# Attention with a threshold, then a squared-ReLU MLP: GpSimd issues the writes of turned blocks, and one piece of MLP work changes sides of the values

## The chip, the cores and the metric

The kernel runs on one core of a Trainium2 chip. The metric is the device time of one execution in microseconds (us). A core has these engines, each with an instruction stream of its own: TensorE (PE in the profile, its weight loads PEld) multiplies matrices, VectorE (DVE) and ScalarE (ACT) do elementwise work and read PSUM, GpSimd (POOL) does elementwise work in SBUF, and SyncE (SP) here only issues DMAs. ACT and POOL can issue DMAs too. Every engine works through its instructions in order, and an instruction that waits holds up everything behind it on its engine.

## The reference

There are 8 batches with 8 heads, 576 tokens and 64 values per head. Each row of scores keeps only the entries within tau of its maximum. The result goes through a two-layer MLP, 512 to 2048 to 512, over all 4608 tokens.

```python
scores = scale * np.matmul(q, k.transpose(0, 1, 3, 2))
thresh = np.max(scores, axis=-1, keepdims=True) - tau
scores = np.where(scores >= thresh, scores, -1000000000.0)
scores = scores - np.max(scores, axis=-1, keepdims=True)
attn = np.exp(scores)
attn = attn / (np.sum(attn, axis=-1, keepdims=True) + 1e-09)
attn_out = np.matmul(attn, v)
x = attn_out.transpose(0, 2, 1, 3).reshape(B * S, H * D)
r = np.maximum(x @ w_in, 0.0)
out = (r * r) @ w_out
```

Everything is float32.

## The kernel before

**Visits and steps.** Two heads of a batch are worked on together; this is a *visit*. There are 36 visits, numbered from 0: the four head pairs of the first batch come twice (a part of the queries each time), the other 28 once. A visit goes through blocks of 128 queries; one block is one *step*. From visit 12 on, visits come in pairs (an even and an odd one) that share nine steps: first a block made of the 64 left-over queries of both, then blocks 0 to 3 of the even visit, then blocks 0 to 3 of the odd one. The odd visit is the "second visit" of the change's description.

**One step.** TensorE computes the scores into PSUM (L289). VectorE takes the row maxima (L310), ScalarE the exponents (L322 to L325), VectorE applies the threshold and sums (L337 to L340), GpSimd divides (L345 and L347) in SBUF.

**Values.** The product with v (`mix`, L502) needs the weights with keys on the partitions. From visit 11 on this is done in three moves. `turn_blocks` transposes 32x32 blocks on VectorE into the tile `turned` (L431 to L441), one step after the weights were divided. For two blocks of queries together `set_aside` (L408) writes 1152 KB of `turned` to `aside`, a buffer in HBM. `place_blocks` reads it back with four DMAs of SP (L449) so that each 32x32 block lies at its place in the tile `wT`. The blocks of left-over queries go from `turned` to `wT` directly (L458, L466). So each full visit has two writes and eight placements; there are 50 writes and 200 placements in all. Only then can the values of the visit be computed: for an even visit four steps after its last step, for an odd one three steps after. The values go to PSUM bank 0 (first group) and bank 4 (second group); the second group needs the blocks that were placed last. ACT copies both banks to `xT` (the puts, L485 to L496).

**MLP.** Work on chunks of 256 tokens is cut into *pieces*, which wait in a queue and fill TensorE between attention steps: `piece()` takes the next one. In chunks from the third on both layers use seven products of half-size blocks instead of eight; L659 is the first layer (`unit`), L765 the second (`product`). Sums and differences of weight blocks for these are made by GpSimd and VectorE (L590), others of tokens by GpSimd (L636), the evictions by ACT and VectorE (among them L671, L691, L803). GpSimd issues the stores of the output (L743).

**Order.** The order on every engine is the program's order, written out by hand. `late_step` is one step of the stretch with pairs. It emits the scores, maxima and exponents; then, if the block turned in this step is the second of two, its transposes and, through `turn_last`, the write. Then come some pieces (`fill` takes them by an estimated share of time), threshold and division, loads, and in a step that has values (`valued`) the three things at issue: `at_least(1, made)` makes sure that a piece lies between what went before and the values, `values()` emits them, and after the placements and further fills `at_least(2, made)` makes sure that two pieces lie between the values and the next scores.

The DMAs that SP issues stand in one order too: loads of q, k and v for later visits (L201), placements (L449, L458, L466).

Of the kernel before, what the change touches and what calls it, by code (L numbers as in the profile page):

```python
# [19 lines left out]
def kernel(  # L20
# [10 lines left out]
    nc = tc.nc  # L31
# [62 lines left out]
    NB = 2 * KB * 2 * 32  # L94
    turned = const.tile([P, 2 * NB], FP32, name="turned")
# [102 lines left out]
    def some_loads():  # L198
        for _ in range(min(1 + (len(loads) > 8), len(loads))):
            to, src = loads.popleft()  # L200
            nc.sync.dma_start(out=to, in_=src)  # L201
# [75 lines left out]
    def area(u, odd):  # L277
        at = AT[u, odd][0]
        return big[:, at:at + S].rearrange("p (h k) -> p h k", h=2)

    def scores_of_two(s):


        vis, i = steps[s]

        def term(u, odd, second_part, lhsT, keys, to=slice(0, P)):
            at, cut = AT[u, odd]
            x0, x1 = (cut, S) if second_part else (0, cut)
            nc.tensor.matmul(big[to, at + x0:at + x1], lhsT, keys[u * D:(u + 1) * D, x0:x1], start=True, stop=True)  # L289

        if i == NBLK:
            for x in range(2):
                for v_ in range(2):
                    for u in range(2):
                        cols = slice(v_ * D, (v_ + 1) * D)
                        term(u, 0, x != u, qmid[u * D:(u + 1) * D, cols], kT[v_], cols)
            return
        for at_, (u, odd, x) in enumerate(((1, 1, 0), (0, 0, 0), (1, 0, 1), (0, 0, 1), (1, 0, 0), (0, 1, 0), (1, 1, 1), (0, 1, 1))):
            at = (i + odd) * P
            term(u, odd, x, qT[u * D:(u + 1) * D, at:at + P], kT[vis % 2])  # L300
            if at_ == 0:
                nc.scalar.copy(seen, big[:, AT[1, 1][0]:AT[1, 1][0] + 1])

    def maxima(s, sc):
        vis, i = steps[s]
        n = len(sc)
        st = stats[s % len(stats)]
        mx = st[:, 0, 0:n]
        for u in range(n):
            nc.vector.tensor_reduce(out=mx[:, u:u + 1], in_=sc[u], axis=AX.XY, op=ALU.max)  # L310
        w = w_slots[(s - first_dma) % (2 if by_dma(vis) else 3)][:, 0:n, :]
        weights[vis, i] = w, sc, st
# [6 lines left out]
    def exponents(vis, i):  # L319
        w, sc, st = weights[vis, i]  # L320
        mx, thr, bias = (st[:, j, 0:len(sc)] for j in range(3))
        nc.scalar.activation(out=bias, in_=mx, func=AF.Copy, scale=-SCALE)  # L322
        nc.scalar.activation(out=thr, in_=mx, func=AF.Identity, bias=ntau8)  # L323
        for u in range(len(sc)):
            nc.scalar.activation(out=w[:, u, :].rearrange("p (h k) -> p h k", h=2), in_=sc[u],  # L325
                                 func=AF.Exp, bias=bias[:, u:u + 1], scale=SCALE)
# [78 lines left out]
    def set_aside(vis, pair):  # L405

        t = aside[len(outside) % 4]
        nc.scalar.dma_start(out=t, in_=turned[:, 0:NB])  # L408
        outside[vis, pair] = t.rearrange("(b r) (j x) -> r j b x", r=32, j=4)

    def turn_blocks(vis, i):
# [31 lines left out]
    def place_blocks(vis, pair, which=range(4)):  # L443

        wb = blocks[vis, pair]
        if pair < NBLK // 2:
            for j in range(4):
                g0 = (ONE, TWO)[pair] // REST
                nc.sync.dma_start(out=wT[j * 32:j * 32 + 32, g0:g0 + 4, :, :].rearrange("r b c q -> r b (c q)"),  # L449
                                  in_=outside[vis, pair][:, j, :, :])  # L450
            return
        for qb in which:
            rows = slice(qb * 32, qb * 32 + 32)
            for j in range(4):
                to = wT[j * 32:j * 32 + 32, :, :, :]
                at = slice(qb % 2 * 32, qb % 2 * 32 + 32)
                if paired(vis):
                    nc.sync.dma_start(out=to[:, (LEFT if qb < 2 else ODD) // REST, :, at], in_=wb[rows, j:2 * KB:4, :])  # L458
                else:


                    first = j if qb < 2 else KB + (j - KB) % 4
                    n = len(range(first, KB if qb < 2 else 2 * KB, 4))
                    c = first // 4
                    first += 2 if qb < 2 else -KB
                    nc.sync.dma_start(out=to[:, LEFT // REST, c:c + n, at], in_=wb[rows, first:first + 4 * n - 3:4, :])  # L466
# [152 lines left out]
    def some_later(engine):  # L619
        if later[engine]:  # L620
            make(*later[engine].popleft())
# [212 lines left out]
    mixes = {}  # L834
# [46 lines left out]
    def add_chunk(j):  # L881
        waiting.extend(pieces_of(j))
        whole.add(j)
# [23 lines left out]
    def after():  # L907
        now = state["last"]
        state["last"] = []
        for fn in state["then"]:  # L910
            state["last"] += fn() or []
        state["then"] = []
        for fn in now:
            fn()

    def piece():
        _, fn, *what = waiting.popleft()
        state["left"] -= PIECE_US
        state["made"] += 1
        if fn is mlp_out or what[0] <= PLAIN and what[1] == 0:  # L920
            after()
        then = fn(*what)
        after()
        state["then"] = then
        if state["step"] >= NST:
            some_later("vector")
            some_later("gpsimd")

    def fill(us):
        state["left"] += us  # L930
        while waiting and state["left"] >= PIECE_US / 2 and waiting[0][0] <= state["usable"]:
            piece()
        state["left"] = min(state["left"], PIECE_US)
# [75 lines left out]
    def turn_last(s):  # L1009
        if s <= NST:  # L1010
            turn_blocks(*steps[s - 1])
            n, i = steps[s - 1]
            if i % 2 and by_dma(n) and goes_out(n, i // 2):
                set_aside(n, i // 2)

    def goes_out(n, pair):

        return pair < NBLK // 2

    def at_least(count, made):  # L1020
        while waiting and state["made"] < made + count:
            piece()

    def late_step(s):

        on = s < NST
        odd = on and steps[s][1] % 2 == 1
        if on:
            n, i = steps[s]
            if not odd:  # L1030
                scores_of_two(s)
            after()
            maxima(s, [area(u, odd) for u in range(2)])
            some_later("gpsimd")
            exponents(n, i)
        first = s > NST or steps[s - 1][1] % 2 == 1 or steps[s - 1][1] == NBLK
        if first:
            turn_last(s)
        valued = s in mixes and s < END

        todo = list(place_at[s])

        def place(all_):
            for what in list(todo):
                if all_ or not goes_out(*what[:2]):
                    place_blocks(*what)
                    todo.remove(what)

        if not valued:
            place(False)  # L1050

        def values():
            if s in mixes:
                while (visits[mixes[s][0]][0] // HP + 1) * S - RING > read_to["x"]:
                    piece()
                mix(*mixes[s])
                for j in chunk_at.get(s, ()):
                    add_chunk(j)

        if s == END:  # L1060
            values()
        quarter = rate(s) / 4 if s < END else 1e9
        made = state["made"]
        fill(quarter)
        some_later("gpsimd")
        after()
        if on:
            threshold(n, i)
            divide(n, i)
        if first:  # L1070
            some_later("vector")
        fill(quarter)
        after()
        if not first:
            some_later("vector")
            turn_last(s)
        for fn in prep_at[s] + load_at[s]:
            fn()
        some_later("gpsimd")
        if valued:  # L1080
            at_least(1, made)
            made = state["made"]
            values()
        some_loads()
        place(True)
        some_later("vector")
        some_loads()
        fill(quarter)
        some_loads()
        fill(quarter)  # L1090
        some_loads()
        if valued:
            at_least(2, made)
            state["left"] = max(state["left"], -PIECE_US / 2)

    for s in range(END + 1):
        state["step"] = s
        if s >= first_late:
            assert 4 not in kept.values()
            late_step(s)  # L1100
            continue
# [137 lines left out]
```

## Time and profile before

| what | value |
|---|---|
| median of 3 runs | 1334.41 us (1334.23 to 1335.61) |
| the profiled execution | 1334.19 us, of which the span of its instructions is 1332.4 us |
| mean granted clock of TensorE | 0.995 |
| writes of turned blocks (L408, ACT queue) | 50 of 1152.0 KB, median 5.2 us from issue to landing |
| placements (L449, SP queue) | 200 of 288.0 KB, median 5.5 us to landing |
| stores of the output (L743, POOL queue) | 32 of 256.0 KB, median 3.3 us to landing |
| HBM read and written | 133 GB/s over the span |

How to read what follows. A row of the timeline has the start, the length, the engine, the line, what is written and read, and how many instructions were merged; a bracket at its end tells how long the engine was idle before it and what ended the wait. A row of waits reads: engine and line, what it waited for, the total in us, how often, the longest. A row of the windows has, for each stretch, the busy time and the number of instructions of each engine, the clock, the DMA engines' share and GB/s. Names with a q (SPq, ACTq) are an engine's sequencer, which issues DMAs. The page's own warning stands: a busy TensorE is not TensorE at its peak, since ends of matmuls are modelled.

### The profile page before, as it was taken

To read this page: it belongs to the slowest core of one execution; us is meant where nothing else is said; L and a number is where in the kernel's file an instruction comes from. 1 tells how busy PE (TensorE), PEld (TensorE's weight loads), DVE (VectorE), ACT (ScalarE), POOL (GpSimd) and SP (SyncE) were. 2 spreads that over 40 slices of the span, in tenths; PEclk is the share of its full clock that TensorE was granted. 3 is DMA by queue.
4 is the path that set the end of the run, shared out by engine and by line. 5 is a ranking of instruction groups with operands and counts; after the bars stand their busy time and mean duration, and the time that the engine had idled before them with its cause. 6 is when DMAs were issued, how large, how long until landed. Compare 5 with 4: busy or idle time off the path is not lost.

```text
span 1332.4 us, 25133 instructions
## 1 busy us (share of the span) xinstructions
PE 1297.2 (97%) x9112; PEld 1078.2 (81%) x9112; DVE 928.2 (70%) x2026; ACT 585.2 (44%) x1357; POOL 758.3 (57%) x865
## 2 busy tenths in 40 slices
PE   7898999999999999999999999999999999999998
PEld 5676556878796979787888888888887888889997
DVE  6877776777787878777786777868687877732131
ACT  4776674235262535343434443444434343422321
POOL 4689875765655555364655554737274737354451
PEclk7999999999999999999999999999999999999999
DMA  8764531647767686867586685758677577430000
GB/s 159 160 152 117 144 91 36 160 93 183 167 177 170 169 195 165 200 141 200 123 186 147 172 192 138 189 108 205 138 181 169 150 180 164 141 91 1 17 17 16
DMA packets 330124, 186.68 MB, mean 140 GB/s; under 512 B 291440, under 2 KB 291472, under 8 KB 323600
## 3 DMA queue, kind: packets, MB, share of 16 engines
q1 hardware_dynamic: 317696, 116.87, 45.0%
q10 hardware_dynamic: 9504, 59.27, 11.2%
q0 software_dynamic: 2800, 8.93, 1.8%
q8 instruction: 72, 1.18, 0.4%
q14 instruction: 52, 0.43, 0.1%
HBM read 109.22 MB, written 68.42 MB: 133 GB/s over the span
## 4 chain that ended last, share of the span: by engine, by line
PE 85%; DVE 5%; ACT 4%; DMA 3%; POOL 2%; issue 1%; SPq 1%; ACTq 0%; DVEq 0%; POOLq 0%
PE big L659 28%; PE big L765 27%; PE big L502 10%; PE big L289 8%; PE big L548 3%; PE big L273 3%; PE big L730 2%; PE big L386 2%; DMA wT<-aside 2%; DVE st L310 1%; DVE w L337 1%; ACT w L325 1%; ACT wT L387 1%; DMA aside<-turned 1%; PE big L266 0%
## 5 line engine op out<-in xcount | busy, mean ns | idle before, releaser
L337 DVE SCALAR_TENSOR_TENSOR w<-big,st,w 128x576 f32<-128x576 f32 x269 | 207.2, 807 | 97.8 <-ACT w L325 97.5
L310 DVE TENSOR_REDUCE st<-big 128x1 f32<-128x576 f32 x288 | 204.3, 748 | 86.2 <-PE big L289 53.5
L347 POOL TENSOR_SCALAR w<-w,st 128x576 f32<-128x576 f32 x269 | 247.4, 929 | 28.0 <-DVE st L340 24.0
L765 PE MATMUL big<-wo,gsum 128*128 128x256 f32 x1088 | 243.8, 382 | 0.0
L345 POOL TENSOR_SCALAR st<-st 128x2 f32<-128x2 f32 (+1 forms) x148 | 36.6, 247 | 358.6 <-DVE w L337 354.2
L765 PEld LDWEIGHTS big<-wo,gsum 128*128 128x128 f32 x1088 | 204.4, 190 | 37.1 <-issue 8.6
L659 PE MATMUL big<-xT,w_in_sb 128*128 128x128 f32 x1536 | 187.3, 277 | 0.8 <-DVE g L671 0.7
L659 PEld LDWEIGHTS big<-xT,w_in_sb 128*128 128x128 f32 x1536 | 178.5, 192 | 9.8 <-issue 7.6
L765 PE MATMUL big<-wo,g 128*128 128x256 f32 x816 | 185.3, 382 | 0.1
L325 ACT ACTIVATE w<-big,st 128x576 f32<-128x576 f32 x269 | 183.8, 734 | 0.2 <-ACT st L323 0.2
L502 PE MATMUL big<-wT,vs 128*64 128x128 f32 (+5 forms) x1700 | 164.8, 355 | 9.7 <-ACT wT L387 4.2
L765 PEld LDWEIGHTS big<-wo,g 128*128 128x128 f32 x816 | 151.6, 190 | 26.1 <-issue 6.5
L502 PEld LDWEIGHTS big<-wT,vs 128*64 128x64 f32 (+1 forms) x1700 | 97.3, 137 | 73.9 <-issue 21.5
L322 ACT ACTIVATE st<-st 128x2 f32<-128x2 f32 (+1 forms) x148 | 30.3, 205 | 263.4 <-DVE st L310 262.2
L671 DVE TENSOR_TENSOR g<-big,g 128x512 f32<-128x512 f32 x96 | 64.8, 677 | 82.3 <-PE big L659 76.4
L289 PE MATMUL big<-kT,qT 64*128 64x320 f32 (+3 forms) x768 | 108.0, 416 | 0.2 <-DVE w L337 0.2
L289 PEld LDWEIGHTS big<-kT,qT 64*128 64x128 f32 x768 | 84.5, 186 | 15.7 <-issue 4.3
L538 POOL TENSOR_TENSOR gsum<-g 128x512 f32<-128x512 f32 x34 | 46.1, 1356 | 81.6 <-ACT g L668 72.1
L667 ACT ACTIVATE g<-g 128x512 f32<-128x512 f32 x96 | 60.3, 628 | 61.0 <-DVE g L671 59.4
L668 ACT ACTIVATE g<-g 128x512 f32<-128x512 f32 x128 | 80.7, 630 | 4.1
L431 DVE STREAM_TRANSPOSE turned<-w 128x512 f32<-128x512 f32 x100 | 70.3, 703 | 3.7 <-DMA aside<-turned 2.6
L437 DVE STREAM_TRANSPOSE turned<-w 128x512 f32<-128x512 f32 x100 | 66.9, 669 | 0.0
(113 smaller groups left out, 1973.2 us busy)
## 6 DMA issues: line engine op xcount, KB each, us to landing
aside<-turned ACTq DMA_DIRECT2D x50, 1152.0 KB, 5.2
wT<-aside SPq DMA_DIRECT2D x200, 288.0 KB, 5.5
vs<-in_v_dram SPq DMA_DIRECT2D x72, 128.0 KB, 4.4
ql<-in_q_dram SPq DMA_DIRECT2D x126, 72.0 KB, 2.9
wo<-in_moe_w_in_dram SPq DMA_DIRECT2D x16, 512.0 KB, 4.8
wo<-in_moe_w_out_dram SPq DMA_DIRECT2D x16, 512.0 KB, 3.7
out_dram<-osb POOLq DMA_DIRECT2D x32, 256.0 KB, 3.3
kl<-in_k_dram SPq DMA_DIRECT2D x113, 72.0 KB, 3.0
```

The lines of the kernel that those rows point to most:

```text
L289: nc.tensor.matmul(big[to, at + x0:at + x1], lhsT, keys[u * D:(u + 1) * D, x0:x1], start=True, stop=True)
L310: nc.vector.tensor_reduce(out=mx[:, u:u + 1], in_=sc[u], axis=AX.XY, op=ALU.max)
L325: nc.scalar.activation(out=w[:, u, :].rearrange("p (h k) -> p h k", h=2), in_=sc[u], func=AF.Exp, bias=bias[:, u:u + 1], scale=SCALE)
L337: nc.vector.scalar_tensor_tensor(out=wu, in0=sc[u], scalar=thr[:, u:u + 1], in1=wu, op0=ALU.is_ge, op1=ALU.mult, accum_out=sm[:, u:u + 1])
L347: nc.gpsimd.tensor_scalar(out=w[:, u, :], in0=w[:, u, :], scalar1=z[:, u:u + 1], scalar2=rcp[:, u:u + 1], op0=ALU.add, op1=ALU.mult)
L431: move(wb[:, 0:h, :, :], whole_[:, 0, :, :, :])
L437: move(wb[:, h + 1:, :, :], whole_[:, 1, :, :, :])
L502: nc.tensor.matmul(ps[u * D:(u + 1) * D, :], vs[n % 2][rows, u * (NBLK + 1) + c, :], wT[rows, at // REST:(at + ps.shape[1]) // REST, NBLK ...
L659: nc.tensor.matmul(to[:, f, :], factor(j, p, q, c)[:, f * P:(f + 1) * P], part[:, c, :], start=(p in "125" and f == 0 and c == 0), stop=(p ...
L668: nc.scalar.activation(out=to, in_=to, func=AF.Square)
L671: nc.vector.tensor_tensor(out=x, in0=to, in1=x, op=ALU.add)
L765: nc.tensor.matmul(to, left[:, f, :], wo[:, slot, f, :], start=(f == 0), stop=(f == HF - 1))
```

## The change

The write of turned blocks is issued by GpSimd instead of ScalarE, at the same place of the program. And in `late_step`, where a step has values, the counts of pieces ahead of and behind them depend on whether the visit is odd: for even visits one piece ahead and two behind, as before; for odd visits (`mixes[s][0] % 2` is 1) two ahead and one behind. `mixes[s]` holds the visit and the query columns whose values step `s` computes.

```diff
     def set_aside(vis, pair):

         t = aside[len(outside) % 4]
-        nc.scalar.dma_start(out=t, in_=turned[:, 0:NB])
+        nc.gpsimd.dma_start(out=t, in_=turned[:, 0:NB])
         outside[vis, pair] = t.rearrange("(b r) (j x) -> r j b x", r=32, j=4)
...
         some_later("gpsimd")
         if valued:
-            at_least(1, made)
+            at_least(1 + mixes[s][0] % 2, made)
             made = state["made"]
             values()
         some_loads()
...
         fill(quarter)
         some_loads()
         if valued:
-            at_least(2, made)
+            at_least(2 - mixes[s][0] % 2, made)
             state["left"] = max(state["left"], -PIECE_US / 2)
```

## The prediction

> **What bounds the kernel now.** I read the page's busy table first, then the table of windows, the timeline around TensorE's waits, and last SP's waits and timeline.
>
> ```profile
> PE 1297.2 (97%) x9112; PEld 1078.2 (81%) x9112; DVE 928.2 (70%) x2026; ACT 585.2 (44%) x1357; POOL 758.3 (57%) x865
> ```
>
> ```profile
> core 0: us, PE busy (x) PEld busy (x) DVE busy (x) ACT busy (x) POOL busy (x), PEclk, DMA share, GB/s
> 243.00:400.00 157.00, 155.50 (x1044) 130.97 (x1044) 122.79 (x271) 65.41 (x153) 98.11 (x110) 1.00 0.67 159
> 400.00:600.00 200.00, 197.21 (x1403) 164.28 (x1400) 157.37 (x354) 83.00 (x196) 112.27 (x132) 1.00 0.73 174
> 600.00:800.00 200.00, 200.00 (x1412) 168.57 (x1413) 151.04 (x336) 84.23 (x194) 112.17 (x130) 1.00 0.71 169
> 800.00:1000.00 200.00, 198.60 (x1395) 170.29 (x1391) 152.00 (x336) 84.05 (x195) 111.99 (x129) 1.00 0.68 160
> 1000.00:1180.00 180.00, 179.84 (x1240) 149.69 (x1239) 131.05 (x288) 70.38 (x164) 98.26 (x113) 1.00 0.66 162
> ```
>
> TensorE is the bound. The change touches only the stretch from 243 us (the first write of turned blocks is issued at 238.8) to 1180 (the last values). There TensorE is idle for 1.50 + 2.79 + 0.00 + 1.40 + 0.16 = 5.85 us of 937. This caps the gain: 5.85 us is 0.44%. POOL is busy for 57% and has room on average. Four of the idle pieces stand before values (L502):
>
> ```profile
> 278.13 4.75 PE L502 MATMUL big<-wT,vs 128*64 128x320 f32 x38 [1.14 <-DMA wT<-turned]
> ...
> 401.56 2.63 PE L502 MATMUL big<-wT,vs 128*64 128x256 f32 x24 [0.26 <-DMA wT<-aside]
> ...
> 425.32 2.63 PE L502 MATMUL big<-wT,vs 128*64 128x256 f32 x24 [1.14 <-DMA wT<-aside]
> 427.88 3.72 PE L765 MATMUL big<-wo,gsum 128*128 128x256 f32 x16
> 431.53 0.92 PE L289 MATMUL big<-kT,qT 64*128 64x256 f32 x4
> ...
> 567.57 2.63 PE L502 MATMUL big<-wT,vs 128*64 128x256 f32 x24 [1.36 <-DMA wT<-aside]
> ```
>
> The brackets are what the change can win: 1.14 + 0.26 + 1.14 + 1.36 = 3.90 us. By the order of the visits these are visits 11, 14, 15 and 19; three are odd. After visit 15's values two pieces of MLP (3.65 us up to the scores at 431.53) stand behind them. Now SP, which places the blocks:
>
> ```profile
> SPq L201 <- DMA aside<-turned: 165.4, 24, 9.7
> SPq L449 <- DMA aside<-turned: 160.4, 15, 31.8
> ...
> SPq L458 <- DMA aside<-turned: 91.1, 11, 9.8
> ```
>
> ```profile
> 449.02 13.36 SPq L201 DMA_DIRECT2D vs<-in_v_dram  x8
> 462.48 0.54 SPq L201 DMA_DIRECT2D kl<-in_k_dram  x1
> 463.06 1.92 SPq L449 DMA_DIRECT2D wT<-aside  x4
> ```
>
> L449 needs the write's data. L201 loads v, k and q and has nothing to do with it; still it waits for it, 165.4 us in 24 waits. In the built program every DMA of SP and ACT takes the next of eight completion semaphores in turn and waits until its last holder has landed; a write sits on one for its whole flight. So the eight v loads take 13.36 us to issue. The write in question was issued at 451.31 and landed 8.78 later, at 460.09, yet its placement starts only at 463.06, behind loads that had been held up.
>
> **What the Trainium skill says.** "DMA: Bandwidth & Descriptors", section "SWDGE vs HWDGE vs iDMA": a DMA from ACT or SP gets its descriptors from hardware, one from GpSimd from software on GpSimd's cores. Section "The descriptor swizzle": a 1 MiB transfer over 128 partitions needs nine read and nine write descriptors per DMA engine. So rows count, not bytes. The trace agrees as far as it goes: output stores from POOL (L743, 128 rows of 2 KB) occupy POOL for 0.56 to 0.60 us. "SBUF — State Buffer", section "SBUF: two separate sides": descriptor writing stalls while VectorE holds the port it shares with GpSimd; in the section "A bandwidth-pool intuition that's wrong" a DMA of some 620 ns alone takes 3100 beside such an operation. No L743 shows that: all 33 lie between 0.56 and 0.80.
>
> **Part 1: the write moves from ACT to GpSimd.**
>
> *Removed from ACT*: 50 issues of 0.33 us, 16 us, on an engine 44% busy: nothing on the path. The write cannot start earlier, since ACT already issues each 0.03 us after the last transpose ends (for instance 411.98 and 412.01).
>
> *Added to POOL*: 50 x 0.6 = 30 us. I compared POOL's state with the end of the transposes for all 50. In 36 POOL is idle then, 34 times with L345 next, which waits for VectorE's threshold still to come; in the other 14 it is in an L590, L539, L559 or L743 that ends within 1.25 us. The tightest POOL work before TensorE is L590 at 910.7 (TensorE waits 0.73 for it at 912.0). The new issue ahead of it falls between POOL's end at 905.53 and the L345 at 906.12, a hole of 0.59. Cost taken: nothing; if that cover fails, up to 0.6 there.
>
> *Later landing*, call it D. Nothing in the trace shows this write from POOL. Nearest rows, output stores of 256 KB near the end of the run, with no other transfers about (first from POOL, then from SP):
>
> ```profile
> L743 POOL DMA_DIRECT2D out_dram<-osb x4: 560/560/560, 1233.3 to 1285.0; - x4
> DMA to landing us min/median/max: 2.3/2.3/2.3
> ...
> L743 SPq DMA_DIRECT2D out_dram<-osb x2: 362/362/362, 1326.9 to 1329.1; - x2
> DMA to landing us min/median/max: 2.0/2.0/2.0
> ```
>
> By the records 2.30 and 2.04 us: D = 0.26. The skill's fit for GpSimd's path (section "Anatomy of one DMA") gives 2.0 + 1.18 MB / 436e3 = 4.7 us for the write's size, an estimate; the quietest writes from ACT take 4.14, so D = 0.56. Upper end: the 2.5 us of the port stall above, with some loss of share beside SP's loads, 3. Lower end 0, as the issue cannot come earlier. I take 0.5.
>
> *Where D lands.* Even visits: SP's loads no longer wait for the write, so the placement starts when the write lands. In all eleven even visits from 12 to 32 the placement started 2.4 to 4.0 us after the landing, 2.97 for visits 14 and 16. That covers D and some more contention from loads that now fly beside the write. Visit 14's wait of 0.26 goes. Odd visits: placement follows landing by 0.05 to 0.07, so D counts in full. The last values (visit 35, at 1178.11) open the final stretch and are not moved by part 2; there TensorE already waits 0.07 for a placement that landed at 1177.98. Cost D, 0.5.
>
> **Part 2: one more piece before the values of odd visits.** In the built program 12 places change, visits 11, 13, ... 33: one piece goes from behind the values to before them. The instructions are the same; no queue but TensorE's is passed, though puts, and SP's placements that wait for these values to be read, come one piece later. A piece is eight L765 passes of 0.216 plus a changeover, or sixteen L659 passes of 0.112: 1.8 us. Visit 11: 1.14 wait, gone with 0.66 to spare; its placement does not come from the write. Visit 15: 1.14 + D against 1.8, gone. Visit 19: 1.36 + 0.5 against 1.8: 0.06 left, nothing. Visit 17 had 0.10 in hand by the landings, the other odd ones 1.2 to 4.0; all gain. Taken: 3.64 for the odd ones and 0.26 for visit 14.
>
> What is late next? The scores behind the values need their two PSUM banks evicted. ACT ends these puts 0.84 to 0.90 after the values in every visit, against 1.8 from one piece: covered by 0.9. If ACT were in a pair of squares then (2 x 0.63), 0.3 each. On VectorE the order changes twice: an L590 (0.75) comes before an L803 that frees a bank. Where TensorE is near that L803 it costs up to 0.75 each; I take 0.4 in all.
>
> **Sum.** -3.90 + 0.5 (end) + 0.4 (VectorE) = -3.0. The profiled execution took 1334.19 (span 1332.4); the median is 0.22 above it. 1334.41 - 3.0 = 1331.4.
>
> **Rivals.**
> 1. *The write from GpSimd lands late.* The place is the odd placements and the last values. TensorE's cost is D at the end, D - 0.66 at visit 15, D - 0.44 at visit 19, and from 1.8 on D - 1.8 at visit 17. It eats the whole 3.9 from D = 1.7 and makes the kernel slower by 0.2% from D = 2.4. At D = 3: 3.0 + 2.3 + 2.6 + 1.2 - 3.9 = +5.2, 1339.6. For it: DMA share is 0.66 to 0.73 here, and writes beside loads already take up to 10.5 us. Against it: POOL's stores keep to 0.6 and the quiet difference is 0.26.
> 2. *The gain is given back.* L743 and the writes now share POOL's order, L590 slips by 0.6 in some chunks (three more chunks have L590 within 1 us of TensorE), puts meet squares, and D is 1.2. D alone then costs 1.2 + 0.5 + 0.8 = 2.5; with 0.5 for the rest, 0.9 of the 3.9 is left: 1333.5.
> 3. *More than the four waits goes.* Earlier k and q loads also take VectorE's 14.0 us of waits for them (L247), and with them TensorE's wait of 0.57 for kT at 778.6; most of the 5.85 goes: 1329.5.
> 4. *The extra piece does nothing because VectorE is late with the scores anyway.* Against it: the landings, not scores, stand in the brackets. Part of rival 2.
>
> **How the numbers follow.** Against 1334.41 a measurement tells a change from none at about 0.2%, 2.7 us, so faster means below 1331.7 and slower above 1337.1. Forecast 50% (own range 1330.2 to 1332.6; 34% faster, 16% same); rival 1 20%, slower (a lesser D is in rival 2); rivals 2 and 4 20%, same; rival 3 10%, faster. Faster 0.44, same 0.36, slower 0.20. Low end 1329.6, about rival 3's; high end 1338.0, inside rival 1. Left out are some 15% above and 5% below.
>
> **What would show it.** L408 on POOL at about 0.6 us x50; landing 4.5 to 5 at the quietest; SP's L201 no longer waits for the write; no TensorE wait at visits 11, 14, 15, 19; a new one of about 0.5 before the last values; idle in this stretch near 3 us. I am wrong if the quietest write takes over 6 us, if L408 holds POOL for over 1.2, or if new waits stand before L289 or L659.

## The result and the profile after

The changed kernel takes 1339.65 us, the median of 6 runs (1338.66 to 1340.28); the kernel before, on the same chip, 1334.24 (1333.31 to 1335.61, 6 runs). The ratio is 1.0031, with a 95% interval of 1.0021 to 1.0041: slower by some 5.4 us, where the forecast was 1331.4, 3.0 us faster. The profiled execution took 1340.09 us, of which the span is 1338.3; before, 1334.19 and 1332.4. What follows is about the 5.9 us between the two spans.

First the page of the kernel after: its busy line, and the groups and the DMA row of the write.

```profile
PE 1297.4 (97%) x9112; PEld 1078.8 (81%) x9112; DVE 924.6 (69%) x2026; ACT 582.7 (44%) x1357; POOL 785.3 (59%) x915
...
L408 POOL DMA_DIRECT2D aside<-turned x50 | 29.9, 597 | 179.8 <-DVE turned L437 177.9
...
aside<-turned POOLq DMA_DIRECT2D x50, 1152.0 KB, 4.7
```

TensorE's busy time has not changed (1297.2 before). The write is on POOL, 50 x 597 ns, and the median from issue to landing is now 4.7 us instead of 5.2. The windows of the kernel after, for the stretch with turned blocks (its last window ends 4 us later than the one of before, since the last values come later):

```profile
core 0: us, PE busy (x) PEld busy (x) DVE busy (x) ACT busy (x) POOL busy (x), PEclk, DMA share, GB/s
243.00:400.00 157.00, 156.62 (x1064) 131.98 (x1066) 123.58 (x279) 65.69 (x153) 105.02 (x119) 1.00 0.74 166
400.00:600.00 200.00, 195.42 (x1377) 162.88 (x1374) 153.07 (x348) 82.08 (x194) 116.12 (x141) 0.99 0.75 173
600.00:800.00 200.00, 200.00 (x1416) 169.72 (x1416) 150.91 (x335) 82.80 (x192) 117.96 (x140) 1.00 0.71 164
800.00:1000.00 200.00, 198.31 (x1393) 169.24 (x1390) 150.92 (x336) 83.14 (x195) 117.90 (x140) 1.00 0.70 161
1000.00:1184.00 184.00, 181.86 (x1256) 151.05 (x1254) 131.37 (x291) 70.95 (x165) 103.70 (x123) 1.00 0.65 159
```

The first window gained (idle 0.38 instead of 1.50). The second lost: 4.58 idle instead of 2.79, at a clock of 0.99. The last lost too, 2.14 instead of 0.16. TensorE's waits in the kernel after say on what (engine and line, what it waited for, total us, how often, the longest; rows that stand alike in both kernels, or nearly so, are left out):

```profile
PE big L659 <- POOL t L636: 4.8, 3, 4.2
...
PE big L659 <- POOL g L590: 1.5, 2, 0.7
...
PE big L502 <- DMA wT<-aside: 1.3, 1, 1.3
```

Before, L502 waited for `wT<-aside` three times, 2.8 us, and for `wT<-turned` once, 1.1; of those four waits none is left. The single wait for `wT<-aside` is a new one, before the last values. The wait for L636 is new altogether. TensorE's timeline around it, kernel after:

```profile
419.75 1.24 PE L765 MATMUL big<-wo,gsum 128*128 128x256 f32 x5
420.92 4.79 PE L502 MATMUL big<-wT,vs 128*64 128x320 f32 x40
425.63 1.99 PE L765 MATMUL big<-wo,gsum 128*128 128x256 f32 x8
427.56 2.21 PE L289 MATMUL big<-kT,qT 64*128 64x256 f32 x16
429.70 3.84 PE L659 MATMUL big<-xT,w_in_sb 128*128 128x128 f32 x32
437.69 4.57 PE L659 MATMUL big<-t,g 128*128 128x128 f32 x24 [4.16 <-POOL t L636]
```

This is visit 15, the same place that the prediction showed of before. The values run through (40 passes in 4.79 us, no wait), one block of eight L765 has gone ahead of them and eight are left behind, as the change wants it. By 427.56 TensorE is 3.97 us ahead of the kernel before. Ten us later it waits 4.16 us for GpSimd's token differences (L636). Now GpSimd in that stretch, first before, then after:

```profile
427.47 1.63 POOL L347 TENSOR_SCALAR w<-w,st 128x576 f32<-128x576 f32 x2 [0.25 <-DVE st L340]
429.07 0.73 POOL L636 TENSOR_TENSOR t<-xT 128x256 f32<-128x256 f32 x1
429.87 0.78 POOL L636 TENSOR_TENSOR t<-xT,t 128x256 f32<-128x256 f32 x1
430.62 0.72 POOL L636 TENSOR_TENSOR xT<-xT 128x256 f32<-128x256 f32 x1
431.30 0.72 POOL L797 TENSOR_TENSOR osb<-held,osb 128x256 f32<-128x256 f32 x1
431.99 2.48 POOL L590 TENSOR_TENSOR g<-g,w_in_sb 128x512 f32<-128x512 f32 x2
```

```profile
426.82 1.10 POOL L797 TENSOR_TENSOR osb<-held,osb 128x256 f32<-128x256 f32 x1 [0.47 <-DVE osb L796]
427.88 2.48 POOL L590 TENSOR_TENSOR g<-g,w_in_sb 128x512 f32<-128x512 f32 x2
430.31 0.63 POOL L743 DMA_DIRECT2D out_dram<-osb  x1
430.97 1.29 POOL L590 TENSOR_TENSOR gsum<-w_in_sb,g 128x512 f32<-128x512 f32 x1
432.57 0.56 POOL L408 DMA_DIRECT2D aside<-turned  x1 [0.31 <-DVE turned L437]
433.14 1.28 POOL L590 TENSOR_TENSOR gsum<-w_in_sb,g 128x512 f32<-128x512 f32 x1
434.35 0.58 POOL L743 DMA_DIRECT2D out_dram<-osb  x1
435.01 0.22 POOL L345 TENSOR_SCALAR st<-st 128x2 f32<-128x2 f32 x1
435.33 1.62 POOL L347 TENSOR_SCALAR w<-w,st 128x576 f32<-128x576 f32 x2
436.92 0.72 POOL L636 TENSOR_TENSOR t<-xT 128x256 f32<-128x256 f32 x1
```

Before, L636 came right behind the division and ahead of L797. After, it stands behind L797, four L590, two stores, the write and another division: one whole step later. GpSimd is not slow here and hardly idle; it has the work in another order.

That wait has a second price, which is no idle time. Windows of the kernel after, on both sides of 438 us:

```profile
434.00:438.00 4.00, 0.30 (x2) 0.31 (x3) 3.57 (x6) 0.00 (x0) 3.74 (x7) 1.00 0.92 323
438.00:442.00 4.00, 4.00 (x24) 4.00 (x23) 0.00 (x0) 1.04 (x2) 4.00 (x5) 0.57 0.42 71
442.00:446.00 4.00, 4.00 (x38) 4.00 (x37) 1.63 (x5) 3.33 (x8) 0.29 (x2) 1.00 0.99 221
```

TensorE is shown busy from 438 to 442, but with 24 passes where the next window has 38, and a granted clock of 0.57. By the clock records it ran at half speed for 3.41 us from 438.33. Half of that, about 1.7 us, is lost. The Trainium skill, "TensorE: Matmul & The Clock Gate", section "What's actually happening", has it so: after an idle window of about 3.4 us the array's clock falls to half. The wait here is longer than that, 4.16 us, and 3.41 us at half speed follow it. Shorter waits in other runs had the same price; the last section has them.

Last, the end of the program: the closing drains of POOL (L1234 is the line that opens and closes the whole program; a row gives the shortest, median and longest in ns, then the first and last start). Before, and then after:

```profile
L1234 POOLq DRAIN  x3: 46/102/3797, 1326.1 to 1332.1; - x3
L1234 SPq DRAIN  x3: 7/7/7, 1331.6 to 1331.9; - x3
```

```profile
L1234 POOLq DRAIN  x3: 46/102/7881, 1329.6 to 1338.0; - x3
L1234 SPq DRAIN  x3: 7/7/7, 1334.7 to 1337.8; - x3
```

GpSimd's long drain takes 7.88 us instead of 3.80. Before, it was over at 1329.9, ahead of SP's first drain at 1331.6, which follows the landing of the last store. After, it runs to 1337.5, when SP has long been through (1334.7): the end now waits for GpSimd.

The 5.9 us as a sum. The rows are differences of the starts of the same score blocks (L289) in the two traces, not brackets, so that stretched and half-speed passes count. The times of L636 and L590 are those of the waits in the kernel after, the others are times in the kernel before:

| stretch | after - before, us |
|---|---|
| start of the stretch (257.5) | +0.30 |
| 265.8 to 286.5: visit 11's values and the scores ahead of them | -3.10 |
| L636 at 293 | +0.53 |
| visit 14's values | -0.48 |
| visit 15's values | -1.22 |
| L636 at 437.7, with the half clock | +6.00 |
| visit 19's values | -1.45 |
| L636 at 580.6 | +0.67 |
| L590 at 1052.8 | +1.33 |
| small ones together | -0.24 |
| last values, to TensorE's end | +1.19 |
| GpSimd's drain, to the end of the span | +2.36 |
| sum | +5.89 |

So the four waits of the forecast went, and with a short one of 0.23 ahead of visit 11's values they brought more than forecast (6.25 us in all), and 12 us of other things came. The experiments ask which part of the change brought which.

### The profile page after: what moved, and what is told of

Its sections match the earlier page's. It is cut to its first block, busy times and chain, and to the rows that moved or that the text cites. A ratio compares the mean times of both kernels' runs of the same rounds, so it can differ in the third digit from the quotient of the medians.

```text
span 1338.3 us, 25217 instructions
## 1 busy us (share of the span) xinstructions
PE 1297.4 (97%) x9112; PEld 1078.8 (81%) x9112; DVE 924.6 (69%) x2026; ACT 582.7 (44%) x1357; POOL 785.3 (59%) x915
## 4 chain that ended last, share of the span: by engine, by line
PE 84%; DVE 5%; POOL 4%; ACT 3%; DMA 2%; issue 1%; SPq 0%; ACTq 0%; POOLq 0%; DVEq 0%
PE big L659 28%; PE big L765 27%; PE big L502 10%; PE big L289 8%; PE big L548 3%; PE big L273 3%; PE big L730 2%; PE big L386 2%; DVE w L337 1%; DVE st L310 1%; ACT w L325 1%; ACT wT L387 1%; POOL w L347 1%; POOL g L590 1%; POOL turned L156 1%
## 5 line engine op out<-in xcount | busy, mean ns | idle before, releaser
L765 PE MATMUL big<-wo,gsum 128*128 128x256 f32 x1088 | 243.8, 382 | 0.0
L765 PEld LDWEIGHTS big<-wo,gsum 128*128 128x128 f32 x1088 | 204.3, 190 | 37.0 <-issue 7.1
L659 PE MATMUL big<-xT,w_in_sb 128*128 128x128 f32 x1536 | 187.2, 277 | 1.1 <-DVE g L671 1.0
L659 PEld LDWEIGHTS big<-xT,w_in_sb 128*128 128x128 f32 x1536 | 178.4, 192 | 9.6 <-issue 7.6
L765 PE MATMUL big<-wo,g 128*128 128x256 f32 x816 | 185.3, 382 | 0.1
L765 PEld LDWEIGHTS big<-wo,g 128*128 128x128 f32 x816 | 151.6, 190 | 26.1 <-issue 7.0
L502 PE MATMUL big<-wT,vs 128*64 128x128 f32 (+5 forms) x1700 | 163.3, 355 | 7.0 <-ACT wT L387 4.2
L502 PEld LDWEIGHTS big<-wT,vs 128*64 128x64 f32 (+1 forms) x1700 | 96.1, 137 | 70.7 <-issue 19.4
L408 POOL DMA_DIRECT2D aside<-turned x50 | 29.9, 597 | 179.8 <-DVE turned L437 177.9
L671 DVE TENSOR_TENSOR g<-big,g 128x512 f32<-128x512 f32 x96 | 64.7, 676 | 80.6 <-PE big L659 74.9
L289 PE MATMUL big<-kT,qT 64*128 64x256 f32 (+3 forms) x768 | 106.8, 416 | 0.0
L289 PEld LDWEIGHTS big<-kT,qT 64*128 64x128 f32 x768 | 84.4, 186 | 14.5 <-issue 4.6
L431 DVE STREAM_TRANSPOSE turned<-w 128x512 f32<-128x512 f32 x100 | 70.2, 702 | 0.0
```

Source lines behind the costliest of these rows:

```text
L431: move(wb[:, 0:h, :, :], whole_[:, 0, :, :, :])
L502: nc.tensor.matmul(ps[u * D:(u + 1) * D, :], vs[n % 2][rows, u * (NBLK + 1) + c, :], wT[rows, at // REST:(at + ps.shape[1]) // REST, NBLK ...
L659: nc.tensor.matmul(to[:, f, :], factor(j, p, q, c)[:, f * P:(f + 1) * P], part[:, c, :], start=(p in "125" and f == 0 and c == 0), stop=(p ...
L671: nc.vector.tensor_tensor(out=x, in0=to, in1=x, op=ALU.add)
L765: nc.tensor.matmul(to, left[:, f, :], wo[:, slot, f, :], start=(f == 0), stop=(f == HF - 1))
```

## The experiments

Part 1 is the write's engine, part 2 the order of pieces. All ratios are to the kernel before, run on the same chip in the same series (median 1335.09 of 20 runs in the first four, 1335.30 of 14 in the fifth and sixth, 1335.29 of 31 in the last two).

| kernel | median us (range) | ratio, 95% interval |
|---|---|---|
| part 1 alone | 1334.94 (1332.82 to 1335.82) | 0.9996, 0.9988 to 1.0004 |
| part 2 alone | 1349.68 (1349.16 to 1350.89) | 1.0109, 1.0096 to 1.0122 |
| both, asking in both halves | 1331.57 (1330.80 to 1333.55) | 0.9972, 0.9960 to 0.9983 |
| part 2, asking in both halves | 1342.81 (1339.13 to 1346.74) | 1.0059, 1.0042 to 1.0076 |
| both, asking, late writes on ScalarE | 1329.93 (1329.10 to 1334.42) | 0.9964, 0.9951 to 0.9977 |
| before, with 50 scattered DMAs on GpSimd | 1529.57 (1526.77 to 1532.52) | 1.1456, 1.1432 to 1.1479 |
| before, with 50 one-row DMAs on GpSimd | 1337.74 (1336.62 to 1339.98) | 1.0025, 1.0016 to 1.0033 |
| part 1 for the early writes alone | 1333.08 (1330.90 to 1334.97) | 0.9979, 0.9973 to 0.9986 |

And what the records of their profiled executions give: TensorE's idle time after 243 us (all gaps), the end of its last pass, what lies behind that up to the end of the span, GpSimd's long drain, and the DMAs that GpSimd issued in the whole program. Each row is one execution. The scores that start at 257.5 us in the kernel before start 0.5 us earlier to 1.6 us later in the others, near the start of the stretch that the change touches, so the ends compare to no better than that.

| kernel | idle | TensorE's end | behind it | drain | DMAs |
|---|---|---|---|---|---|
| before | 5.8 | 1328.50 | 3.89 | 3.80 | 36 |
| after | 8.8 | 1332.03 | 6.25 | 7.88 | 86 |
| part 1 alone | 4.8 | 1327.32 | 6.26 | 7.88 | 86 |
| part 2 alone | 15.7 | 1343.48 | 3.90 | 3.80 | 36 |
| both, asking | 4.6 | 1325.50 | 6.25 | 7.88 | 86 |
| part 2, asking | 10.6 | 1337.10 | 3.90 | 3.80 | 36 |
| both, asking, late writes on ScalarE | 3.5 | 1324.66 | 3.96 | 5.59 | 58 |
| before, one-row DMAs | 6.6 | 1329.34 | 6.53 | 7.88 | 86 |
| part 1, early writes alone | 4.5 | 1325.17 | 3.96 | 5.59 | 58 |

**Part 1 alone.** Only the changed line of `set_aside`.

> Part 1 alone (GpSimd issues the writes, pieces as before). Theory A (three separate costs: late token differences through part 2, GpSimd's final drain, the last values): TensorE's wait of 4.2 us for L636 near 437 us is absent; GpSimd's final drain lasts about 7.9 us as in the changed kernel, end of the program later by 2.4; a wait of about 1.2 before the last values; waits at visits 11, 15 and 19 of 1.1, 1.7 and 2.0. Sum +2.4 + 1.2 + 1.2 - 0.3 = +4.5, about 1338.8. Theory B (GpSimd's issues and late landings make the whole loss, also the 4.2): the 4.2 wait is there too, 1343 or more.

1334.94: no change that can be measured, and neither of the two numbers that were expected. The later landing costs next to nothing. At the two odd visits where it had to show in full, the waits are 1.25 and 1.39 us, against 1.14 and 1.36 before, and the last values do not wait at all. So a late landing does not explain the result. Nor do POOL's 30 us: no wait for L636, and the one for L590 at 0.73 as before. But the drain is there (6.26 us behind TensorE's end). The waits before visits 11 and 14 are gone without part 2. Part 1 gains in the middle, above all at 266 to 286 us, and pays it out at the end.

**Part 2 alone.** Only the two changed lines of `late_step`.

> Part 2 alone (ScalarE issues the writes, one more piece before the values of odd visits). Theory A: the wait for L636 near 437 us stays at 3.5 to 4.2, those near 293 and 580 at 0.2 to 0.4, the waits at visits 11, 15 and 19 are gone, the final drain is back at 3.8 us and the last values wait under 0.1: -3.6 + 4.4 = +0.8, about 1335. Theory B: nothing is left but the gain, about 1330.6.

1349.68, slower by far than before, than the whole change and than either number expected. The late L636 is here too, 3.71 us at 441.9, with the half clock behind it (0.58 in the window from 442 to 446), and no write on GpSimd anywhere near. So it is part 2 that brings it. A second wait, of 5.29 us, is of another kind. The scores behind it start 7.2 us later for it, since 6.83 us at half clock begin within it. TensorE and then SP's queue in this kernel:

```profile
547.45 2.38 PE L502 MATMUL big<-wT,vs 128*64 128x320 f32 x16
555.12 4.37 PE L502 MATMUL big<-wT,vs 128*64 128x256 f32 x24 [5.29 <-DMA wT<-aside]
```

```profile
541.14 10.55 SPq L449 DMA_DIRECT2D wT<-aside  x4
551.74 1.51 SPq L201 DMA_DIRECT2D kl<-in_k_dram  x3
```

Four placements take 10.55 us to issue. By the records three go out from 541.14 to 542.59 and the fourth at 551.39, 0.01 us after the *next* write has landed at 551.38. It is the ring of eight completion semaphores: the fourth placement's turn falls on the semaphore that this write holds, and the values of an even visit wait for a write that they do not need. The order of the pieces decides which DMA gets which place in the ring. With the write on GpSimd that trap cannot shut: in the trace of the kernel after, GpSimd's DMAs hold semaphores 99 to 106, while SP's go round 107, 108 and 110 to 115.

**Both parts, with the asking put right.** The next chunk's token differences T1 to T3 are asked for in `product`, in the first half of its fifth to seventh product, if the chunk is already complete (`whole`: its values have been added). A piece is half a product. Where the piece that part 2 moves ahead of the values is such a first half, and these values complete the chunk, the question comes too early, and the second half behind the values does not ask again. At 437.7 us it was the last product of its chunk, so that the next to ask was the first piece of the next chunk itself, two pieces before the answer was needed. This kernel asks in both halves:

```diff
-        if x >= 4 and not half and j + 1 in whole:
+        if x >= 4 and j + 1 in whole:
             ask((j + 1, "T1"), (j + 1, "T2"), (j + 1, "T3"))
```

> Both parts, and a product asks for the next chunk's token differences in its second half too. Theory A: L636 comes back to its old place in GpSimd's order, the waits of 4.2, 0.4 and 0.3 go, drain (7.9) and last values (1.2) stay: 1339.65 - 4.8 = 1334.9. Theory B: the wait stays, as the write stands in the way of L636: 1339.7.

1331.57, where 1334.9 was the lower of the two numbers expected. TensorE and GpSimd at the same place as above:

```profile
433.07 3.74 PE L659 MATMUL big<-t,g 128*128 128x128 f32 x32
437.79 2.05 PE L659 MATMUL big<-xT,w_in_sb 128*128 128x128 f32 x16 [0.99 <-DVE g L671]
```

```profile
430.02 0.72 POOL L636 TENSOR_TENSOR t<-xT 128x256 f32<-128x256 f32 x1
430.82 0.73 POOL L636 TENSOR_TENSOR t<-xT,t 128x256 f32<-128x256 f32 x1
431.50 0.74 POOL L636 TENSOR_TENSOR xT<-xT 128x256 f32<-128x256 f32 x1
```

L636 is back at 430.0, TensorE does not wait for it, and the clock stays at full. The waits at 293, 580 and 1052.8 are gone as well. All of them hung on the missed question. By the starts of scores in the two traces they cost 7.2 us with the half clock; by the medians, 1339.65 against 1331.57, some 8. The drain and a wait of 1.71 us before the last values have stayed.

**Part 2 alone, asking in both halves.** Part 2 alone with the same edit of `product`.

> Part 2 alone, with the asking in both halves of a product. Theory A: waits at visits 11, 15, 19 gone, no new wait above 0.5, drain 3.8, last values under 0.1: 1334.24 - 3.6 = 1330.6. Theory B: like part 2 alone, both 1330.6.

1342.81, where both theories had 1330.6. The late L636 is gone, the trap in the ring is not: 3.19 us before visit 18's values, and 2.22 before visit 12's. Both are followed by 3.41 us at half clock. Thus part 2 with the asking put right costs 7.7 us without part 1 (1342.81 - 1335.09), and brings 3.4 with it (1331.57 - 1334.94). The two parts cannot be priced one by one and added.

**Both parts, asking, and the later writes by ScalarE again.** If the drain grows with the number of GpSimd's DMAs, fewer of them must shorten it.

```diff
-        nc.gpsimd.dma_start(out=t, in_=turned[:, 0:NB])
+        (nc.gpsimd if vis < 22 else nc.scalar).dma_start(out=t, in_=turned[:, 0:NB])
```

> As the kernel with both parts and the second asking, but ScalarE issues the writes of visits 22 to 35 (28 writes); GpSimd keeps 22. GpSimd then issues 58 DMAs in all. If its final drain grows with their number (3.80 us at 36, 7.88 at 86, so 0.082 each), it lasts 5.6 us and is hidden behind SP's last store: 2.4 us gained, less up to 0.6 of new waits where SP's placements of late visits share semaphores with writes again: 1329.2 to 1329.8. If the drain does not depend on the number, it stays at 7.9 and the time at 1331.6. The wait before the last values: if a late landing from GpSimd made it, it is under 0.3 now that ScalarE issues that write; if not, it stays at 1.3 to 1.7.

1329.93, below both kernels and close to what was expected. The drain, by the same view as above:

```profile
L1234 POOLq DRAIN  x3: 46/102/5590, 1322.2 to 1328.4; - x3
```

5.59 us with 58 DMAs, and only 3.96 us lie behind TensorE's end. A new wait of 0.86 us (for L691 of ACT, at 781 us) takes a part of it back. The last values do not wait here. By the test set out above that would speak for a late landing from GpSimd; but part 1 alone has this write on GpSimd and does not wait either, and both kernels with part 2 on ScalarE do. The issuer does not decide it.

**The drain by itself, first attempt.** The kernel before, its writes on ScalarE, and one small DMA of GpSimd more behind each. `note` is a scratch tensor in HBM, made for this run and read by nothing.

```diff
         nc.scalar.dma_start(out=t, in_=turned[:, 0:NB])
+        nc.gpsimd.dma_start(out=note, in_=ntau8)
```

> The kernel before, where GpSimd issues an additional DMA of 512 bytes after each of ScalarE's 50 writes, into a scratch tensor that nothing reads. If the final drain counts DMAs: 7.9 us, and the program ends 2.4 us later, 1334.24 + 2.4 = 1336.6, with TensorE's waits as before. If it counts bytes or flight: 3.8 us and 1334.3. If GpSimd's 30 us of issues cost TensorE time by themselves, new waits stand before L659.

The drain takes 7.88 us, as the count says. The time does not answer: 1529.57. The DMA chosen was a column, 128 pieces of 4 bytes, and these DMAs took 10.7 us to land in the median. The write's row of this kernel's page:

```profile
aside<-turned ACTq DMA_DIRECT2D x50, 1152.0 KB, 10.3
```

With fifty DMAs of 512 bytes more, the landing of the writes rose from 5.2 to 10.3 us. (The page's median has only the 12 writes whose landing it can pair with their issue; by the last update of each write's semaphore it is 9.5 over all 50.) The price of the drain could not be read from this run.

**The drain by itself, second attempt.** The same with one row of 512 bytes in one piece (`note` has that shape here).

```diff
         nc.scalar.dma_start(out=t, in_=turned[:, 0:NB])
+        nc.gpsimd.dma_start(out=note[0:1, :], in_=ident[0:1, :])
```

> The kernel before, writes of turned blocks still by ScalarE, and behind each of the 50 GpSimd issues a DMA of one row of 512 bytes, so that no scatter of small elements stands in the other transfers' way as in the run before. Theory (GpSimd's closing drain is paid by the number of DMAs that it issued): the drain takes 7.9 us instead of 3.8, SP's last store is no longer the end, the end is 2.4 us later: 1336.5 to 1337.7; POOL takes some 0.6 us for each of the 50 issues and TensorE's waits in the middle stay those of the kernel before. Rival (the drain grew for another reason, such as the bytes of the turned blocks): drain 3.8, 1334.2 to 1335.5. Second rival (POOL's 30 us of issues cost by themselves): drain 7.9 and new TensorE waits of over 1 us behind L590 or L636.

1337.74, at the upper edge of what the first theory expected. The write lands after 5.5 us, nearly as before (5.2), and the drain:

```profile
L1234 POOLq DRAIN  x3: 46/102/7876, 1326.9 to 1335.6; - x3
```

Its length counts DMAs, not bytes: 50 rows of 512 bytes lengthen it just as 50 writes of 1152 KB do. The same holds, nearly, of POOL's time for an issue: 547 ns for one row here, 597 for the 128 rows of a write. 6.53 us lie behind TensorE's end. The 50 issues left TensorE's waits nearly as they were, 6.6 us in all.

**Part 1 for the early writes alone.** Part 1 alone with the condition `vis < 22`.

> Part 1 alone, but only for visits up to 21 (22 of the 50 writes by GpSimd, 28 by ScalarE). Theory: the drain takes 3.80 + 22 x 0.082 = 5.6 us and ends about as SP's last store lands, so nearly the whole 2.36 us that the drain costs in part 1 alone is saved: 1332.4 to 1333.6, if the waits of TensorE stay as in part 1 alone (1334.94). Rival (the drain is covered or something else ends last): 1334.5 to 1335.5.

1333.08, as expected: two us below part 1 alone. The waits before visits 15 and 19 (1.26 and 1.38 us) and the total idle time are nearly those of part 1 alone; what differs is the 2.3 us behind TensorE's end. (The two ends of TensorE also lie 2.1 us apart, but as much stood between these two executions at 257 us already.)

## Why the prediction was wrong

**The step that failed** is in part 2: "The instructions are the same; no queue but TensorE's is passed". That the instructions are the same is true. But the program lets work of other engines depend on where a piece stands: a first half of a product asks for token differences, and whether it does hangs on which values have been added by then. One piece ahead, and GpSimd's L636 comes a step later. That is a term of 7 to 8 us that the sum does not have, and with it away the kernel takes 1331.57, 3.5 us below its own base, beside a forecast of 1331.4 and 3.0 below. That nearness is partly luck, since three more terms were off:

- **The gain** was sized at 3.90 us, by the brackets. It was 6.25. All four waits went, as forecast, and a fifth of 0.23 with them. Visits 14, 15 and 19 gave 0.48, 1.22 and 1.45, near their brackets (0.26, 1.14, 1.36). But the stretch from 265.8 to 286.5 gave 3.10 for brackets of 0.23 and 1.14. TensorE there, kernel before:

```profile
265.76 0.70 PE L289 MATMUL big<-kT,qT 64*128 64x256 f32 x2
266.69 2.51 PE L289 MATMUL big<-kT,qT 64*128 64x384 f32 x14 [0.23 <-DVE w L337]
...
276.24 0.75 PE L502 MATMUL big<-wT,vs 128*64 128x320 f32 x2
```

Two passes of each block went ahead, one behind the other, and are shown busy for 0.70 and 0.75 us; a pair that runs side by side in the same blocks takes about 0.25. The bracket begins only where they are shown to end. From the start of the scores to the next work it is 3.37 us, in part 1 alone 2.14; for the values 6.57 against 4.93. So the two brackets stood for 1.23 and 1.64 us. Both are gone with part 1 alone, 2.87 us over the stretch, though the prediction gave visit 11's wait to part 2.

- **The end of the program** stood nowhere in the prediction. Part 1's issues cost nothing on POOL while it runs, as forecast: 29.9 us, no wait. Yet each GpSimd DMA adds 4.08 / 50 = 0.082 us to the closing drain, and from some 58 of them on it decides the end: 2.36 us.
- **VectorE's order** was put at 0.4. With the asking put right one wait of 0.99 for L671 is left at 437.8, 1.2 us by the starts of scores. VectorE's L590 ahead of that L671 took 2.75 us there, beside two L590 and the write of GpSimd, against 0.67 in the kernel before at this place. No run took the two apart, so the cause stays open.

**D**, the later landing, was a fair size and had less weight. The quietest write from GpSimd took 4.4 us instead of 4.14, and the issue stood 0.30 behind the last transpose instead of 0.03: together about 0.57, forecast 0.5. But amid the loads the landings became quicker (4.7 for 5.2 in the median), and the odd visits of part 1 alone waited only 0.03 to 0.11 longer.

**The last values** were to wait for D, 0.5; they waited 1.25, and the cause is another. Part 1 alone, with the same issuer, does not wait there, while both kernels with part 2 on ScalarE do (1.61 and 1.37). In every trace but that with the scattered DMAs the last write's data is done 5.5 to 6.0 us after issue. Where there is a wait, 15 of its 16 completions come by 6.4 and the last at 7.55 to 8.09; its closing packet, on one of the 16 DMA engines, ends just when a 16 KB fetch of instructions ends that took 1.05 to 1.08 us (6.54 and 6.53 us after issue in the kernel after). Where there is none, all completions are in by 6.42. So it looks as if the fetch came first on that engine, by the chance of its time: the traces without the wait have such a fetch too, and it starts 5.35 to 5.60 us after the issue there, 5.44 to 5.97 where there is a wait. No run here moved the fetch, so this cause is argued, not shown.

**The ring of semaphores** was right. L201 no longer waits for the write; SP's waits in the kernel after, where that row was first:

```profile
SPq L449 <- DMA aside<-turned: 295.5, 44, 32.3
...
SPq L201 <- DVE kT L247: 58.8, 11, 7.9
```

What was not seen is that the same ring shuts on the values themselves once part 2 shifts the order and ScalarE keeps the writes.

**The rivals.** Rival 1, the late landing, has the measured time almost to the digit (1339.6), and is refuted by part 1 alone. Rival 2, the gain given back, is nearest in kind, but with other creditors. Rival 3, that more than the four waits go, is true in part. A fifth wait went, worth 1.23 us, and so did VectorE's waits for q and k (L247). But TensorE's 0.57 for kT, which the rival names, did not (0.56 in the kernel after; it is a gap of the weight loads, not of the passes), and some 5.0 of the 6.25 us are the four waits, worth more than their brackets. Rival 4, that the extra piece does nothing, is refuted: with the asking put right, part 2 takes 3.4 us off part 1 alone. Of what was to prove the forecast wrong, "new waits before L289 or L659" is what came.

## What to carry to other kernels

When a piece of work is moved in a hand-written order, look not only at the instructions that move but at what its place decides: what it asks for, frees or counts, and on which engine that is queued; compare the order of every engine around the few places that changed, not the counts. GpSimd pays for its DMAs at the end of the program too, so look at its closing drain (SP's stays at 7 ns with over 900 DMAs). And read a wait's worth from when the next steps start, not from its bracket: passes that run alone or stand still are shown as busy, and the clock may fall after a wait.

## What the runs showed of the hardware

- GpSimd's closing drain: 3.80 us with 36 DMAs issued by GpSimd in the program, 5.59 with 58, 7.88 with 86, whether the added DMAs are of 512 bytes or of 1152 KB.
- Half clock for 3.41 us came after waits of 4.16, 3.71 and 3.19 us, and for 6.83 us from within the wait of 5.29. It also came for 3.41 us after waits of 2.22 (part 2, asking) and 1.98 (at 822.7 us, with the scattered DMAs), which are shorter than the idle window of the skill's page. After waits of 2.16 and 1.71 there was none, so the length of a wait alone does not decide.
- Its place in time counts too. In each trace the stretches of half clock start on one grid of 3.413 us (with the scattered DMAs for instance at 270.60, 345.69 and 410.55, 22 and 19 steps apart). In the step before each fall from full clock TensorE was idle for 1.98 us or more; of the wait of 2.16 us, 2.01 lay in one step and the rest in the step before it. So by these traces the limit lies near 2.0 us of idle time within one step, and crossing it costs about 1.7 us at once.
- Fifty DMAs of 128 pieces of 4 bytes from SBUF to HBM, 25 KB in all, raised the landing of 1152 KB writes from 5.2 to 10.3 us (9.5 over all 50) and the kernel's time by 14.6%. Fifty of the same size in one piece: 5.5 us, and 0.25%, which is the drain.
- The write from GpSimd occupied it for 555 to 627 ns in all 50 cases; the stall of such an issue beside VectorE's port that the prediction bounded at 2.5 us did not occur once, and no write took over 7.6 us to land.
